# Two chunks of k ahead of ssm_k, four products on GpSimd, 512-column cosine products and a deferred spectrum step

## Chip, cores, metric

The kernel runs on one core of a Trainium2 chip. The metric is device time of one execution in microseconds (us); lower is better. The kernel before has a median of 221.08 us over 3 runs (220.58 to 221.51). Profiles give a span some 2 us shorter than the time (in the profiled run of the changed kernel 221.3 against 223.38).

## The reference, cut

```python
k_pad = jnp.pad(k, ((0, 0), (ks - 1, 0), (0, 0)))                  # B, S, D = 1, 2048, 512; ks = 4
for t in range(ks):                                                  # short causal filter: the "taps"
    k_shift = k_shift + k_pad[:, t:t + S, :] * shift_k[:, ks - 1 - t][None, None, :]
kv = k_shift * v
kv_f = rfft(pad(kv, S)); kf_f = rfft(pad(ssm_k, S))                  # length 4096, along the sequence
y = irfft(kv_f * kf_f)[:, :S] + kv * ssm_D                           # cut: casts and transposes
h = x + layernorm(x) * y                                             # x = q
h2 = h + relu(layernorm(h) @ w1) @ w2                                # Dff = 1376
```

The Fourier transforms are matrix products in two stages with sine and cosine tables. Everything below concerns the first third: loads, taps, transposes, the spectrum of ssm_k, and the start of the product of both spectra.

Names used below: in the profile PE is TensorE (PEld its weight loads), DVE, ACT and POOL are VectorE, ScalarE and GpSimd, and SPq is the queue that issues the loads. A bank is one of the buffers into which TensorE writes its sums. k0 to k3 and v0 to v3 are the four chunks of 512 tokens of k and v; a load "lands" when its data is there. kvx is k after the taps, times v; kfl and xfl are ssm_k and kvx after the transposes. A halved window is a stretch in which the records show TensorE's clock at half.

## The kernel before: the parts concerned

```python
psum = pl.push("psF", bufs=8, space=PSUM)                            # eight one-bank buffers
...
warm = psum.tile([P, CH], F32, tag="ps", name="warm")
for _ in range(11):
    nc.tensor.matmul(out=warm[:], lhsT=wz[:, 0:P], rhs=wz[:], start=True, stop=True)
for c, src in ((0, "k"), (0, "s"), (0, "v"), (1, "k"), (1, "v"), (2, "k"), (2, "v"), (3, "k"), (3, "v")):
    ...   # "s": ssm_k, a plain load; "k" and "v": transposing loads of 512 tokens, all on one queue
...
def taps(u):                                     # 16 units: chunk c of k, quarter rg of the columns
    c, rg = divmod(u, DC)
    ps = psum.tile([P, CH], F32, tag="ps", name="pkv")
    for j in range(KS):
        nc.tensor.matmul(out=ps[:], lhsT=wdiag[:, rg, j, :], rhs=kT[:, rg, CH * c + 16 - j:CH * c + CH + 16 - j],
                         start=(j == 0), stop=(j == KS - 1))
    return u, ps
# times_v(u, ps): kvx = ps * vT on DVE, which frees the bank
...
first = [taps(u) for u in range(4)]
for q in range(8):                               # 64 transposes of ssm_k, copied to kfl by DVE and ACT
    to_rows(lambda n: skv[:, :, :, n], q, kfl, "DDDDADDA"[q])
    if q == 1:
        for u, ps in first:
            times_v(u, ps)
...
for gb in range(8):                              # the other 12 units, between the groups of ssm_k's first stage
    for u in ((4, 5), (6,), (7, 8), (9,), (10, 11), (12,), (13, 14), (15,))[gb]:
        times_v(*taps(u))
    group_k(gb)                                  # 128 short products in four banks, then four copies
...
for q in range(8):                               # 64 transposes of kvx, copied to xfl
    to_rows(lambda n: kvc[:, n // 4, :, n % 4], q, xfl, "DDADDADD"[q])

def spectrum_k(kp):                              # ssm_k's second stage: 16 steps
    ks = slice(2 * kp, 2 * kp + 2)
    ps = [psum.tile([P, 2, 256], F32, tag="ps", name=f"ps2k{s}") for s in range(2)]
    for s in range(2):
        stage2(ps[s], lambda c: a1k[:, c, :], kp, s)     # four 256-column products each
    nc.vector.tensor_tensor(out=kf[:, 0, :, ks], in0=ps[0][:].rearrange("p k j -> p j k"), in1=dcol, op=ALU.add)
    nc.scalar.copy(out=kf[:, 1, :, ks], in_=ps[1][:].rearrange("p k j -> p j k"))

for gb in range(8):                              # two steps, then a group of kv's first stage
    spectrum_k(2 * gb)
    spectrum_k(2 * gb + 1)
    stage1(gb, xfl, lambda o, j, n: a1x[:, o, :, j:j + n], "ADAD", 2 if gb == 7 else 1)
```

GpSimd makes the table cn as eight negated pieces of cs, and last the small tables dre and dim. `a1x` overwrites `a1k` in place, so a group must wait for the spectrum steps that read its columns.

## Time and profile before

| | before |
|---|---|
| time, 3 runs | 221.08 us (220.58 to 221.51) |
| profiled span, mean granted clock | 218.7 us, 0.990 |
| landings k0, ssm_k, v0, k1, v1, k2, v2, k3, v3 | 6.5, 12.2, 14.5, 17.0, 20.3, 22.5, 24.7, 28.6, 32.0 us |
| transposes of kvx start | 36.98 us |
| first add of the spectrum | 41.55 us |
| first product of both spectra (t) on DVE | 65.04 us |

The prediction shows the page's shares and the stages. Two readings are added here. First, the page's row of the granted TensorE clock, one digit for each fortieth of the span (5.5 us), 9 or above being full:

```profile
PEclk9969999999999999999999999999999999999999
```

One slice is reduced: the clock records put a halved window at 13.1 to 16.5 us, inside the transposes of ssm_k (the only other begins at 217.9, where the program ends). Second, the marks by which the stages are compared later, from the timeline (start, length, engine, line, operation, count, and in brackets the idle time before it and what ended it): the transposes of kvx, DVE's copies of them to xfl, the first add of the spectrum, the first t.

```profile
36.98 3.77 PE L217 MATMUL pst<-ident,kvx 128*128 128x128 bf16 x64 [0.17 <-PE ps L244]
37.66 3.97 DVE L221 TENSOR_SCALAR xfl<-pst 128x512 int32<-128x512 int32 x6
41.55 1.42 DVE L330 TENSOR_TENSOR kf<-ps2k,dtab 128x512 fp32r<-128x512 f32 x2
65.04 4.08 DVE L365 TENSOR_TENSOR t<-u,kf 128x704 fp32r<-128x704 f32 x5 [1.27 <-ACT usb L361]
```

From kvx to t the kernel takes 65.04 - 36.98 = 28.06 us, of which 4.57 go to the first add.

### The profile page before, as it was taken

To read this page: it belongs to the slowest core of one execution; us is meant where nothing else is said; L and a number is where in the kernel's file an instruction comes from. 1 tells how busy PE (TensorE), PEld (TensorE's weight loads), DVE (VectorE), ACT (ScalarE), POOL (GpSimd) and SP (SyncE) were. 2 spreads that over 40 slices of the span, in tenths; PEclk is the share of its full clock that TensorE was granted. 3 is DMA by queue.
4 is the path that set the end of the run, shared out by engine and by line. 5 is a ranking of instruction groups with operands and counts; after the bars stand their busy time and mean duration, and the time that the engine had idled before them with its cause. 6 is when DMAs were issued, how large, how long until landed. Compare 5 with 4: busy or idle time off the path is not lost.

```text
span 218.7 us, 7281 instructions
## 1 busy us (share of the span) xinstructions
PE 202.8 (93%) x3103; PEld 139.4 (64%) x3122; DVE 148.2 (68%) x304; ACT 127.7 (58%) x242; POOL 65.9 (30%) x99
## 2 busy tenths in 40 slices
PE   7879889999979999989987899999999999999993
PEld 2276446999968999879965587444444444444442
DVE  7978868899979999957968779742973257130032
ACT  2587858788867888858966699003740066206500
POOL 6059920000029999969200120210021002000000
PEclk9969999999999999999999999999999999999999
DMA  6999960000000000059970000332022110421012
GB/s 96 383 224 191 142 136 7 3 4 3 6 3 0 1 0 3 1 134 216 305 252 3 6 0 3 42 77 55 24 52 63 42 47 0 96 57 42 0 42 54
DMA packets 30383, 15.40 MB, mean 70 GB/s; under 512 B 25520, under 2 KB 29072, under 8 KB 30224
## 3 DMA queue, kind: packets, MB, share of 16 engines
q1 hardware_dynamic: 29520, 14.76, 29.9%
q8 instruction: 24, 0.39, 0.8%
q10 hardware_dynamic: 832, 0.20, 0.4%
q14 instruction: 7, 0.06, 0.1%
HBM read 7.08 MB, written 2.10 MB: 42 GB/s over the span
## 4 chain that ended last, share of the span: by engine, by line
PE 83%; ACT 6%; DMA 4%; issue 2%; DVE 2%; SPq 1%; ACTq 0%
PE ps2m L568 17%; PE ps1m L556 16%; PE pz L482 8%; PE psi L449 7%; PE psy L375 7%; PE pst L217 5%; PE ps L244 4%; PE pkv L271 4%; PE ps2k L259 4%; DMA pre<-in_A_ssm_k_dram 4%; PE ps2k L261 3%; PE u L259 3%; PE u L261 3%; ACT ecore L143 1%; SPq L121 1%
## 5 line engine op out<-in xcount | busy, mean ns | idle before, releaser
L556 PE MATMUL ps1m<-hlnT,w 128*128 128x512 bf16 (+3 forms) x219 | 39.5, 336 | 0.3
L558 ACT ACTIVATE h1T<-ps1m 128x512 bf16<-128x512 f32 (+3 forms) x55 | 27.4, 514 | 21.2 <-PE ps1m L556 20.3
L568 PE MATMUL ps2m<-w,h1T 128*128 128x512 bf16 (+3 forms) x177 | 38.9, 366 | 0.7 <-issue 0.3
L570 DVE TENSOR_TENSOR o<-ps2m,xh 128x512 bf16<-128x512 f32 (+1 forms) x17 | 11.1, 659 | 38.1 <-PE ps2m L568 37.6
L556 PEld LDWEIGHTS <-w 128*128 128x128 bf16 (+1 forms) x220 | 21.7, 100 | 17.6 <-issue 1.4
L568 PEld LDWEIGHTS <-h1T 128*128 128x128 bf16 (+1 forms) x187 | 17.6, 98 | 21.2 <-issue 3.1
L365 DVE TENSOR_TENSOR t<-u,kf 128x704 fp32r<-128x704 f32 x32 | 26.7, 887 | 2.9 <-ACT usb L361 2.6
L365 POOL TENSOR_TENSOR t<-usb,kf 128x320 fp32r<-128x320 f32 x32 | 28.1, 922 | 1.4 <-ACT usb L361 1.0
L493 ACT CAST zt<-pz 128x512 bf16<-128x512 f32 x16 | 8.4, 592 | 29.2 <-PE pz L482 29.2
L482 PE MATMUL pz<-bp,ecore 32*32 32x128 f32 x1024 | 22.5, 384 | 2.3 <-issue 1.4
L231 ACT CAST a<-ps 128x512 fp32r<-128x512 f32 (+1 forms) x42 | 21.2, 575 | 4.3 <-PE ps L244 4.2
L502 POOL TENSOR_SCALAR rstd<-mv 128x4 f32<-128x4 f32 (+1 forms) x7 | 1.6, 232 | 70.3 <-DVE mv L509 70.3
L482 PEld LDWEIGHTS pz<-bp,ecore 32*32 32x32 f32 x1024 | 14.2, 103 | 9.4 <-issue 5.4
L231 ACT CAST kf<-psy 128x512 fp32r<-128x512 f32 x30 | 17.4, 640 | 1.7 <-PE psy L375 0.2
L233 DVE CAST a<-ps 128x512 fp32r<-128x512 f32 (+1 forms) x26 | 16.1, 647 | 3.1 <-PE ps L244 2.9
L507 DVE BATCH_NORM_STATS2 st<-xh 128x6 f32<-128x512 bf16 x28 | 17.4, 680 | 0.0
L449 PE MATMUL psi<-dre,kf 128*128 128x256 f32 x64 | 15.5, 284 | 0.9 <-ACT kf L231 0.9
L375 PE MATMUL psy<-t,ipos 128*128 128x512 f32 x48 | 15.8, 391 | 0.0
L271 PE MATMUL pkv<-kT,wdiag 128*128 128x512 bf16 x56 | 14.8, 380 | 0.8 <-DMA kT<-in_A_k_dram 0.3
L449 PE MATMUL psi<-dim,kf 128*128 128x256 f32 x64 | 15.4, 283 | 0.0
L209 POOL TENSOR_SCALAR c2n<-c2s 128x512 fp32r<-128x512 f32 x8 | 11.9, 1559 | 8.9 <-ACT c2s L177 8.9
L449 PEld LDWEIGHTS psi<-dre,kf 128*128 128x128 f32 x64 | 12.3, 192 | 1.3 <-ACT kf L231 1.3
(115 smaller groups left out, 377.0 us busy)
## 6 DMA issues: line engine op xcount, KB each, us to landing
pre<-in_A_ssm_k_dram SPq DMA_DIRECT2D x1, 2048.0 KB, 8.7
out_dram<-o SPq DMA_DIRECT2D x58, 32.0 KB, 1.6
xh<-in_A_q_dram SPq DMA_DIRECT2D x4, 384.0 KB, 6.8
w<-in_B_w_dram SPq DMA_DIRECT2D x1, 1376.0 KB, 12.7
w<-in_B_w_dram SPq DMA_DIRECT2D x1, 1280.0 KB, 15.8
xh<-in_A_q_dram SPq DMA_DIRECT2D x4, 128.0 KB, 2.8
hlnT<-hln SPq DMA_TRANSPOSE x12, 2.4
w<-in_B_w_dram SPq DMA_DIRECT2D x1, 96.0 KB, 15.4
```

The costliest lines, as they stand in the source:

```text
L231: nc.scalar.copy(out=o, in_=i)
L233: nc.vector.tensor_copy(out=o, in_=i)
L259: nc.tensor.matmul(out=ps[:, kk, :], lhsT=w_re[:, k1, :], rhs=a_in(col(k1, 0)), start=True, stop=False, skip_group_check=True)
L271: nc.tensor.matmul(out=ps[:], lhsT=wdiag[:, rg, j, :], rhs=kT[:, rg, CH * c + 16 - j:CH * c + CH + 16 - j], start=(j == 0), stop=(j == KS ...
L365: eng.tensor_tensor(out=t[:, :, j, :], in0=in0.unsqueeze(1).to_broadcast([P, 2, n, 2]), in1=kfr[:, :, j, ks], op=ALU.mult)
L375: nc.tensor.matmul(out=psy[:], lhsT=m_[:], rhs=t_.rearrange("p j k -> p (j k)"), start=first, stop=not first)
L449: nc.tensor.matmul(out=ps[:, i, :], lhsT=kf[:, c, 4 * m:4 * m + 4, :].rearrange("p r k -> p (r k)"), rhs=d[:].rearrange("p a b -> p (a b)" ...
L482: nc.tensor.matmul(out=pz[32 * a:32 * a + 32, r4, l4, :], lhsT=ecore[rows, rho, n2, :], rhs=rhs, start=(rho == 0), stop=(rho == 1), tile_p ...
L507: nc.vector.bn_stats(out=st[:, t % 4, :], in_=xh[:, t, :])
L556: nc.tensor.matmul(out=ps1[:fsz, :], lhsT=w1[:, c, fc * P:fc * P + fsz], rhs=hlnTs[sc][:, c, part], start=(c == 0), stop=(c == DC - 1))
L558: nc.scalar.activation(out=h1s[sc][:fsz, fc, part], in_=ps1[:fsz, :], func=ACT.Relu)
L568: nc.tensor.matmul(out=ps2[:], lhsT=h1s[sc][:ksz, fc, i * P:(i + 1) * P], rhs=w2[:ksz, fc, ds], start=(fc == 0), stop=(fc == NFC - 1))
```

## The change

The intent: TensorE stands idle until ssm_k lands (2.08 us ahead of 12.29). With k0 and k1 both loaded before it, eight units of taps instead of four fill that time. Their eight banks must be freed before the transposes: ACT copies four of them out and GpSimd multiplies those by v. In the spectrum, the two products that use the cosine table become one of 512 columns, so a step needs one tile of two banks; and its last step ("the spare eighth") goes behind kv's last group, for which `a1` gets eight more columns.

The core of the diff; left out are renamed buffers, the split of the memory for partial sums into two pools (psS, psX), the placing of t and of a later table in spare space, the second half of the cosine table, now made ahead of the transposes, the dealing of the copies of ssm_k's groups (eight letters "AADAAADA" become "ADAADADA"), and kv's last group, which is no longer cut in two:

```diff
-    for c, src in ((0, "k"), (0, "s"), (0, "v"), (1, "k"), (1, "v"), (2, "k"), (2, "v"), (3, "k"), (3, "v")):
+    for c, src in ((0, "k"), (1, "k"), (0, "s"), (1, "v"), (0, "v"), (2, "k"), (2, "v"), (3, "k"), (3, "v")):
...
-    first = [taps(u) for u in range(4)]
+    first = [taps(u) for u in range(8)]
+    ck = early.tile([P, DC, CH], F32, name="ck")
+    for u, ps in first[0:4]:
+        nc.scalar.copy(out=ck[:, u, :], in_=ps)
...
     for h in range(8):
         nc.gpsimd.tensor_single_scalar(out=cn[:, hs, :], ...)
-        if h == 0:
+        if h == 1:
+            for u in range(4):
+                times_v(u, ck[:, u, :], nc.gpsimd)
+        if h == 7:
             nc.gpsimd.tensor_copy(out=dtab[:], ...)
...
-        to_rows(lambda n: skv[:, :, :, n], q, kfl, "DDDDADDA"[q])
+        to_rows(lambda n: skv[:, :, :, n], q, kfl, "DDDDDDAA"[q])
         if q == 1:
-            for u, ps in first:
+            for u, ps in first[4:8]:
                 times_v(u, ps)
...
-        for u in ((4, 5), (6,), (7, 8), (9,), (10, 11), (12,), (13, 14), (15,))[gb]:
+        for u in ((8, 9), (10,), (11,), (), (12,), (13,), (14,), (15,))[gb]:
...
-        ps = [psum.tile([P, 2, 256], F32, tag="ps", name=f"ps2k{s}") for s in range(2)]
-        for s in range(2):
-            stage2(ps[s], lambda c: a1k[:, c, :], kp, s)
+        ps = psK.tile([P, 2, 2, 256], F32, tag="pk", name="ps2k")          # psK: two buffers
+        for kk in range(2):
+            k1 = 2 * kp + kk
+            both = a1k.rearrange("p (o c k) j -> p o k c j", c=2, k=4)[:, k1 // 4, k1 % 4]
+            nc.tensor.matmul(out=ps[:, kk], lhsT=cc[:, k1, :], rhs=both, start=True, stop=False, ...)
+            nc.tensor.matmul(out=ps[:, kk, 0], lhsT=cs[:, k1, :], rhs=a1k[:, col(k1, 1), :], ...)
+            nc.tensor.matmul(out=ps[:, kk, 1], lhsT=cn[:, k1, :], rhs=a1k[:, col(k1, 0), :], ...)
...
         spectrum_k(2 * gb)
-        spectrum_k(2 * gb + 1)
-        stage1(gb, xfl, lambda o, j, n: a1x[:, o, :, j:j + n], "ADAD", 2 if gb == 7 else 1)
+        if gb < 7:
+            spectrum_k(2 * gb + 1)
+        stage1(gb, xfl, lambda o, j, n: a1x[:, o, :, j:j + n], "ADAD", ...)
+    spectrum_k(15)
```

More of the change, by code (lines that the diff above doesn't have):

```diff
@@ L90, with bank @@
     kvp = pl.push("kvp", side="right")
-    psum = pl.push("psF", bufs=8, space=PSUM)
+    psS = pl.push("psS", bufs=4, space=PSUM)
+    psX = pl.push("psX", bufs=4, space=PSUM, side="right")
+    turn = [0]
+    def bank():
+        turn[0] += 1
+        return (psX if turn[0] % 8 in (1, 2, 3, 4) else psS).tile([P, 512], F32, tag="ps", name="ps")[:]
     wsh = consts.tile([P, DC, KS], BF16, name="wsh")
     nc.sync.dma_start(out=wsh[:], in_=A_shift_k.rearrange("(r p) j -> p r j", p=P))
-    pre = slotA.tile([P, 4096 + 2048], I32, tag="A", name="pre")
+    pre = slotA.tile([P, 4096 + 2 * 2048], I32, tag="A", name="pre")
     skf = pre[:, 0:4096].bitcast(BF16)
@@ L110 @@
     nc.vector.memset(wz[:], 1.0)
-    warm = psum.tile([P, CH], F32, tag="ps", name="warm")
+    warm = bank()
     for _ in range(11):
-        nc.tensor.matmul(out=warm[:], lhsT=wz[:, 0:P], rhs=wz[:], start=True, stop=True)
+        nc.tensor.matmul(out=warm, lhsT=wz[:, 0:P], rhs=wz[:], start=True, stop=True)
     nc.vector.memset(kT[:, :, 0:16], 0.0)
-    for c, src in ((0, "k"), (0, "s"), (0, "v"), (1, "k"), (1, "v"), (2, "k"), (2, "v"), (3, "k"), (3, "v")):
+    for c, src in ((0, "k"), (1, "k"), (0, "s"), (1, "v"), (0, "v"), (2, "k"), (2, "v"), (3, "k"), (3, "v")):
         ts = slice(CH * c, CH * c + CH)
@@ L159 @@
     nc.gpsimd.iota(r3[:], pattern=[[1, 64]], base=0, channel_multiplier=0)
-    r2 = early.tile([P, 32, 64], I32, name="w_r")
-    nc.gpsimd.iota(r2[:], pattern=[[2, 32], [128, 64]], base=1, channel_multiplier=0)
+    r2 = pre[:, 6144:8192].rearrange("p (k n) -> p k n", n=64)
+    nc.gpsimd.iota(r2, pattern=[[2, 32], [128, 64]], base=1, channel_multiplier=0)
     n1c = early.tile([P, 1], F32, name="n1c")
@@ L178, in table, with taps, times_v @@
                                  scale=hsc[:, dp:dp + 1], bias=hbi[:, dp:dp + 1])
+    kvx = early.tile([P, 16, DC, 32, 4], BF16, name="kvx")
+    def taps(u):
+        c, rg = divmod(u, DC)
+        ps = bank()
+        for j in range(KS):
+            nc.tensor.matmul(out=ps, lhsT=wdiag[:, rg, j, :], rhs=kT[:, rg, CH * c + 16 - j:CH * c + CH + 16 - j],
+                             start=(j == 0), stop=(j == KS - 1))
+        return u, ps
+    def times_v(u, ps, eng=nc.vector):
+        c, rg = divmod(u, DC)
+        split = "p (a h l) -> p a h l"
+        eng.tensor_tensor(out=kvx[:, :, rg, 8 * c:8 * c + 8, :].rearrange("p h a l -> p a h l"),
+                                in0=ps.rearrange(split, h=16, l=4),
+                                in1=vTs[c][:, rg, :].rearrange(split, h=16, l=4), op=ALU.mult)
     t1 = early.tile([P, 64], I32, name="f1_t")
@@ L192 @@
     _sin(dsc[:], t3[:], 64)
+    first = [taps(u) for u in range(8)]
+    ck = early.tile([P, DC, CH], F32, name="ck")
+    for u, ps in first[0:4]:
+        nc.scalar.copy(out=ck[:, u, :], in_=ps)
     tsn = pre[:, 4096:6144].rearrange("p (k n) -> p k n", n=64)
-    _turns(nc, tsn, r2[:], n2c[:], 8192, False)
+    _turns(nc, tsn, r2, n2c[:], 8192, False)
     table(cs, tsn)
@@ L201 @@
     nc.vector.tensor_copy(out=f1lo[:], in_=f1d[:])
-    _turns(nc, r2[:], r2[:], n2c[:], 8192, True)
-    table(cc, r2[:], (0,))
+    _turns(nc, r2, r2, n2c[:], 8192, True)
+    table(cc, r2)
     dtab = consts.tile([P, 8, DC, 8], BF16, name="dtab")
@@ L209 @@
         nc.gpsimd.tensor_single_scalar(out=cn[:, hs, :], in_=cs[:, hs, :].bitcast(F32), scalar=-1.0, op=ALU.mult)
-        if h == 0:
+        if h == 1:
+            for u in range(4):
+                times_v(u, ck[:, u, :], nc.gpsimd)
+        if h == 7:
             nc.gpsimd.tensor_copy(out=dtab[:], in_=d0[:].rearrange("p r (o g) -> p o r g", g=8))
     def to_rows(cols, q, fl, eng):
-        pst = psum.tile([P, 8, P], BF16, tag="ps", name="pst")
+        pst = bank().bitcast(BF16).rearrange("p (i x) -> p i x", i=8)
         for i in range(8):
@@ L221, in to_rows @@
             nc.vector.tensor_single_scalar(out=fl[:].rearrange("p g d n c -> p g d (n c)").bitcast(I32)[:, :, :, qs],
-                                           in_=pst[:].bitcast(I32).rearrange("p i (d g) -> p g d i", d=2),
+                                           in_=pst.bitcast(I32).rearrange("p i (d g) -> p g d i", d=2),
                                            scalar=0, op=ALU.bitwise_or)
@@ L233, in copy, with stage1 @@
             nc.vector.tensor_copy(out=o, in_=i)
-    def stage1(gb, fl, a_out, engs, parts=1):
-        n = 8 // parts
-        for h in range(parts):
-            pss = [psum.tile([P, n, 64], F32, tag="ps", name=f"ps1_{r}") for r in range(4)]
+    def stage1(gb, fl, a_out, engs, get):
+        n = 8
+        for h in range(1):
+            pss = [get().rearrange("p (g c) -> p g c", g=8) for r in range(4)]
             for gi in range(n):
@@ L248, in stage1 @@
                 copy(engs[(4 * gb + rg) % len(engs)], a_out(gb, 8 * rg + n * h, n),
-                     pss[rg][:].rearrange("p g c -> p c g"))
+                     pss[rg].rearrange("p g c -> p c g"))
     def col(k1, c):
@@ L262, in stage2 @@
                              skip_group_check=True)
-    kvx = early.tile([P, 16, DC, 32, 4], BF16, name="kvx")
-    def taps(u):
-        c, rg = divmod(u, DC)
-        ps = psum.tile([P, CH], F32, tag="ps", name="pkv")
-        for j in range(KS):
-            nc.tensor.matmul(out=ps[:], lhsT=wdiag[:, rg, j, :], rhs=kT[:, rg, CH * c + 16 - j:CH * c + CH + 16 - j],
-                             start=(j == 0), stop=(j == KS - 1))
-        return u, ps
-    def times_v(u, ps):
-        c, rg = divmod(u, DC)
-        split = "p (a h l) -> p a h l"
-        nc.vector.tensor_tensor(out=kvx[:, :, rg, 8 * c:8 * c + 8, :].rearrange("p h a l -> p a h l"),
-                                in0=ps[:].rearrange(split, h=16, l=4),
-                                in1=vTs[c][:, rg, :].rearrange(split, h=16, l=4), op=ALU.mult)
     def group_k(gb):
-        stage1(gb, kfl, lambda o, j, n: a1k[:, :, 32 * o + j:32 * o + j + n], "AADAAADA")
-    first = [taps(u) for u in range(4)]
+        stage1(gb, kfl, lambda o, j, n: a1k[:, :, 32 * o + j:32 * o + j + n], "ADAADADA", bank)
     kfl = early.tile([P, 32, 2, 64, 2], BF16, name="kfl")
@@ L289 @@
     for q in range(8):
-        to_rows(lambda n: skv[:, :, :, n], q, kfl, "DDDDADDA"[q])
+        to_rows(lambda n: skv[:, :, :, n], q, kfl, "DDDDDDAA"[q])
         if q == 1:
-            for u, ps in first:
+            for u, ps in first[4:8]:
                 times_v(u, ps)
-    table(cc, r2[:], (1,))
     dre = consts.tile([P, 2, P], F32R, name="dre")
@@ L299 @@
     nc.gpsimd.memset(dim[:].bitcast(F32), 0.0)
-    a1 = slotA.tile([P, 64 * 256], F32R, tag="A", name="a1")
-    a1k = a1[:].rearrange("p (c j) -> p c j", j=256)
-    a1x = a1[:].rearrange("p (o c j) -> p o c j", o=8, j=32)
+    a1 = slotA.tile([P, 72 * 256], F32R, tag="A", name="a1")
+    a1k = a1[:, 8 * 256:72 * 256].rearrange("p (c j) -> p c j", j=256)
+    a1x = a1[:, 0:64 * 256].rearrange("p (o c j) -> p o c j", o=8, j=32)
     for gb in range(8):
-        for u in ((4, 5), (6,), (7, 8), (9,), (10, 11), (12,), (13, 14), (15,))[gb]:
+        for u in ((8, 9), (10,), (11,), (), (12,), (13,), (14,), (15,))[gb]:
             times_v(*taps(u))
@@ L316 @@
     kvc = kvx[:].rearrange("p h r a l -> p h (r a) l")
+    turn[0] = 0
     for q in range(8):
@@ L322 @@
     kf = slotB.tile([P, 2, 256, 32], F32R, tag="B", name="kf")
+    pl.pop("psX")
+    psK = pl.push("psK", bufs=2, space=PSUM, side="right")
     dcol = dtab[:].rearrange("p o r g -> p (o r g)").unsqueeze(2).to_broadcast([P, 256, 2])
@@ L326, in spectrum_k @@
         ks = slice(2 * kp, 2 * kp + 2)
-        ps = [psum.tile([P, 2, 256], F32, tag="ps", name=f"ps2k{s}") for s in range(2)]
-        for s in range(2):
-            stage2(ps[s], lambda c: a1k[:, c, :], kp, s)
-        nc.vector.tensor_tensor(out=kf[:, 0, :, ks], in0=ps[0][:].rearrange("p k j -> p j k"), in1=dcol, op=ALU.add)
-        nc.scalar.copy(out=kf[:, 1, :, ks], in_=ps[1][:].rearrange("p k j -> p j k"))
+        ps = psK.tile([P, 2, 2, 256], F32, tag="pk", name="ps2k")
+        for kk in range(2):
+            k1 = 2 * kp + kk
+            both = a1k.rearrange("p (o c k) j -> p o k c j", c=2, k=4)[:, k1 // 4, k1 % 4]
+            nc.tensor.matmul(out=ps[:, kk], lhsT=cc[:, k1, :], rhs=both, start=True, stop=False,
+                             skip_group_check=True)
+            nc.tensor.matmul(out=ps[:, kk, 0], lhsT=cs[:, k1, :], rhs=a1k[:, col(k1, 1), :], start=False, stop=True,
+                             skip_group_check=True)
+            nc.tensor.matmul(out=ps[:, kk, 1], lhsT=cn[:, k1, :], rhs=a1k[:, col(k1, 0), :], start=False, stop=True,
+                             skip_group_check=True)
+        nc.vector.tensor_tensor(out=kf[:, 0, :, ks], in0=ps[:, :, 0].rearrange("p k j -> p j k"), in1=dcol, op=ALU.add)
+        nc.scalar.copy(out=kf[:, 1, :, ks], in_=ps[:, :, 1].rearrange("p k j -> p j k"))
     for gb in range(8):
         spectrum_k(2 * gb)
-        spectrum_k(2 * gb + 1)
-        stage1(gb, xfl, lambda o, j, n: a1x[:, o, :, j:j + n], "ADAD", 2 if gb == 7 else 1)
-    pl.pop("psF")
+        if gb < 7:
+            spectrum_k(2 * gb + 1)
+        stage1(gb, xfl, lambda o, j, n: a1x[:, o, :, j:j + n], "ADAD",
+               lambda: psS.tile([P, 512], F32, tag="ps", name="ps")[:])
+    spectrum_k(15)
+    pl.pop("psK")
+    pl.pop("psS")
     pl.pop("xfp")
     prod = pl.push("prod", bufs=3, side="right")
-    psum = pl.push("psP", bufs=2, space=PSUM)
+    psU = pl.push("psU", bufs=2, space=PSUM)
+    psY = pl.push("psY", bufs=2, space=PSUM, side="right")
     ipos = prod.tile([P, P], F32R, name="ipos", bufs=1)
@@ L356, in product @@
         for s in range(2):
-            u = psum.tile([P, 2, 256], F32, tag=f"u{s}", name=f"u{s}")
+            u = psU.tile([P, 2, 256], F32, tag=f"u{s}", name=f"u{s}")
             stage2(u, lambda c: a1x[:, :, c, :], kp, s)
@@ L361, in product @@
             nc.scalar.copy(out=usb[:], in_=uj[:, po, :])
-            t = prod.tile([P, 2, 256, 2], F32R, tag=f"t{s}", name=f"t{s}")
+            if kp % 3 < 2:
+                t = prod.tile([P, 2, 256, 2], F32R, tag=f"t{s}", name=f"t{s}", bufs=2)[:]
+            else:
+                o = 64 * 256 + 1024 * s
+                t = a1[:, o:o + 1024].rearrange("p (a j k) -> p a j k", a=2, k=2)
             for eng, in0, j in ((nc.vector, uj[:, dv, :], dv), (nc.gpsimd, usb[:], po)):
@@ L372, in finish @@
         for s, (a, b, m) in enumerate(((tr[:, 0], ti[:, 1], ineg), (tr[:, 1], ti[:, 0], ipos))):
-            psy = psum.tile([P, 512], F32, tag=f"psy{s}", name=f"psy{s}")
+            psy = psY.tile([P, 512], F32, tag=f"psy{s}", name=f"psy{s}")
             for m_, t_, first in ((ipos, a, True), (m, b, False)):
@@ L385 @@
         finish()
-    pl.pop("psP")
+    pl.pop("psU")
+    pl.pop("psY")
     pl.pop("prod")
@@ L423, in ec_product @@
         nc.gpsimd.iota(r4[:], pattern=[[16, 4], [1, 4], [64, 32]], base=4 * q, channel_multiplier=0)
-        ect[q] = [tmpc.tile([P, 4, 4, 32], I32, tag=f"ec_t{c}", name="ec_t", bufs=4) for c in range(2)]
+        ect[q] = [bpx[:, 16384 + 512 * q:16384 + 512 * q + 512].bitcast(I32).rearrange("p (a l n) -> p a l n", a=4, l=4),
+                  tmpc.tile([P, 4, 4, 32], I32, tag="ec_t", name="ec_t", bufs=4)[:]]
         for c in range(2):
-            nc.gpsimd.tensor_scalar(out=ect[q][c][:], in0=r4[:], scalar1=k1o[:], scalar2=(6144.0, 4096.0)[c],
+            nc.gpsimd.tensor_scalar(out=ect[q][c], in0=r4[:], scalar1=k1o[:], scalar2=(6144.0, 4096.0)[c],
                                     op0=ALU.mult, op1=ALU.add)
@@ L430, in ec_turns @@
         for c in range(2):
-            nc.vector.tensor_single_scalar(out=ect[q][c][:], in_=ect[q][c][:], scalar=8191, op=ALU.bitwise_and)
+            nc.vector.tensor_single_scalar(out=ect[q][c], in_=ect[q][c], scalar=8191, op=ALU.bitwise_and)
     def ec_sin(q, c):
-        _sin(ecore[:, c].rearrange("p (a q l) n -> p q a l n", a=4, l=4)[:, q], ect[q][c][:], 8192, neg=c == 1)
+        _sin(ecore[:, c].rearrange("p (a q l) n -> p q a l n", a=4, l=4)[:, q], ect[q][c], 8192, neg=c == 1)
     def row_stats(mv, t):
@@ L438, in row_stats @@
         nc.vector.bn_aggr(out=mv[:, t, :], in_=st[:, t % 4, :])
+    bpx = slotA.tile([P, 72 * 256], F32, tag="A", name="bp")
+    bp = bpx[:, 0:64 * 256].rearrange("p (m r d n) -> p m r d n", m=64, r=2, d=2)
     for q in range(4):
         ec_product(q)
-    bp = slotA.tile([P, 64, 2, 2, 64], F32, tag="A", name="bp")
     for b in range(32):
```

## The prediction

> **What bounds the kernel now.** I read the page's shares first, then the chain that ended last, then busy time by stretch, then the timeline of the first 68 us, where the change lies.
>
> From the page: TensorE carries the span, so a gain must shorten TensorE's work or its waits.
>
> ```profile
> PE 202.8 (93%) x3103; PEld 139.4 (64%) x3122; DVE 148.2 (68%) x304; ACT 127.7 (58%) x242; POOL 65.9 (30%) x99
> PE 83%; ACT 6%; DMA 4%; issue 2%; DVE 2%; SPq 1%; ACTq 0%
> ```
>
> Busy time by stretch (length; then PE, weight loads, DVE, ACT, POOL; granted clock; DMA share; GB/s). The reader is to see the one TensorE hole (10.2 to 12.3), the reduced clock just after it, a stretch to 37 that is TensorE work with small gaps, and a spectrum stretch (40.5 to 62.2) where DVE is nearly full too.
>
> ```profile
> 10.20:12.30 2.10, 0.01 (x2) 0.01 (x1) 2.00 (x2) 2.10 (x2) 0.00 (x0) 1.00 1.13 283
> 12.30:18.50 6.20, 6.20 (x63) 6.20 (x64) 5.05 (x9) 4.20 (x4) 5.07 (x5) 0.72 1.19 234
> 18.50:37.00 18.50, 16.32 (x556) 8.87 (x564) 14.05 (x22) 13.94 (x25) 10.37 (x15) 1.00 0.75 114
> 37.00:40.50 3.50, 3.50 (x63) 3.50 (x64) 3.36 (x6) 3.12 (x7) 0.00 (x0) 1.00 0.00 0
> 40.50:62.20 21.70, 21.67 (x615) 20.19 (x613) 19.79 (x32) 18.27 (x31) 0.00 (x0) 1.00 0.02 4
> 67.40:95.40 28.00, 27.17 (x170) 24.07 (x168) 25.72 (x32) 23.87 (x57) 26.39 (x35) 1.00 0.00 1
> ```
>
> Timeline (start, length): four units of taps, the wait for ssm_k, the next load issues, and DVE standing for the last chunk of v.
>
> ```profile
> 6.58 3.62 PE L271 MATMUL pkv<-kT,wdiag 128*128 128x512 bf16 x16 [0.27 <-DMA kT<-in_A_k_dram]
> 12.29 6.47 PE L217 MATMUL pst<-ident,pre 128*128 128x128 bf16 x64 [2.08 <-DMA pre<-in_A_ssm_k_dram]
> 16.49 3.46 SPq L121 DMA_TRANSPOSE kT<-in_A_k_dram  x1
> 24.40 3.87 SPq L123 DMA_TRANSPOSE vT<-in_A_v_dram  x1
> 32.09 0.69 DVE L278 TENSOR_TENSOR kvx<-pkv,vT 128x512 bf16<-128x512 f32 x1 [0.97 <-DMA vT<-in_A_v_dram]
> ```
>
> The trace's landing records give k0 6.5, ssm_k 12.2, v0 14.5, k1 17.0, v1 20.3, k2 22.5, v2 24.7, k3 28.6, v3 32.0. From 3.5 to about 32 the DMA engines have work nearly without a break: the first 32 us are a load stream of fixed total length.
>
> Timeline of the spectrum: DVE's add and ACT's copy of one step overlap; 256-column products start 0.12 us apart. Matmuls of 512 columns (third and fourth line) start 0.23 apart.
>
> ```profile
> 60.68 0.28 PE L259 MATMUL ps2k<-a,c2c 128*128 128x256 f32 x1
> 60.80 0.28 PE L261 MATMUL ps2k<-a,c2s 128*128 128x256 f32 x1
> 67.38 0.39 PE L375 MATMUL psy<-t,ipos 128*128 128x512 f32 x1
> 67.61 0.40 PE L375 MATMUL psy<-t,ineg 128*128 128x512 f32 x1
> 60.88 0.69 ACT L331 CAST kf<-ps2k 128x512 fp32r<-128x512 f32 x1
> 60.98 1.28 DVE L330 TENSOR_TENSOR kf<-ps2k,dtab 128x512 fp32r<-128x512 f32 x2
> 63.92 0.36 PE L259 MATMUL u<-a,c2c 128*128 128x256 f32 x1 [0.98 <-DVE a L233]
> ```
>
> [...]the window from 9.7 to 13.1 was 38% busy and the next one, to 16.5, ran at half clock; that is why the 64 transposes took 6.47 us there and 3.77 us at 37. [...]so a doubled matmul saves almost nothing. The trace: 0.12 and 0.23 us. [...]Before, add and copy read separate banks and overlap. [...]The landings above are in order of issue.
>
> **The change, part by part.**
>
> *Loads.* The order becomes k0, k1, ssm_k, v1, v0, k2, v2, k3, v3. k1 ahead of ssm_k costs one transpose load, 2.2 to 2.5 us apiece by the issue times and the landing steps, so ssm_k lands at about 14.6 instead of 12.2, v1 at 16.9, v0 at 20.3. k2 is sixth in both orders and v3 last: they still land at about 22.5 and 32.
>
> *Taps.* A unit is 4 matmuls, 0.85 us at full clock. Units 4 to 7 (3.4 us) move into the hole before ssm_k: TensorE works from 6.6 to about 13.5. The transposes then start at 14.6 at full clock. Their fourth to seventh banks need v1's products on DVE (16.9 + 4 x 0.69 = 19.7), so TensorE ends them at about 20.2 (18.5 before) and DVE the kfl copies at about 22.4. ACT's four copies (0.57 each) and four sine halves (2.1 each) run from 7.5 to about 19.2, before its two kfl pieces.
>
> *Behind that.* Eight units and eight groups are left. One group costs 0.61 of matmuls and 0.42 of gap: 1.03. Before: 18.51 + 12 x 0.85 + 8 x 1.03 = 36.95, as the trace has it. After, unit 8 needs k2: 22.5 + 8 x 0.85 + 8 x 1.03 = 37.5. So the moved work does not return: TensorE stands from 20.2 to 22.5 instead. A second limit is v3 on DVE: 32.0 + four products (0.69) + the four to six copies (0.69) between them also gives about 37.6. The kvx transposes start 0.6 to 0.7 later than at 36.98; DVE, with two copies of the last group behind its last product instead of one, starts theirs about 1.3 later.
>
> *Spectrum.* Per k1, four products of 0.121 = 0.484 become 0.228 + 2 x 0.121 = 0.470: 0.014 x 32 = 0.45 us of TensorE in all. DVE needs per group 2 x 0.68 + 2 x 0.645 = 2.65 of the 2.72 us period. The scheduled instructions show ACT's copy now waiting for DVE's add, as both read both banks. With two buffers of two banks, a buffer is free about 0.06 + 0.66 us later; followed through two groups this still gives 2.7 to 2.75 us a group. No gain here, no loss.
>
> *Spare eighth.* The last spectrum step (0.94) moves behind the last stage-1 group, into the gap of which 0.98 is shown as a wait for DVE. But DVE's last add and ACT's last copy then stand ahead of the first product: their 0.66 each take back most of it. I count 0.7 to 1.0 us of the late start as recovered. The product stage stays at its 1.86 us a step on TensorE.
>
> *Sum.* Late by 1.3 at the kvx copies, less about 1.0: +0.3 us. To this comes the clock: the window from 19.9 to 23.4 would hold 0.3 + 0.85 us of TensorE work, 33%[...]. A halved window at 23.4 to 26.8, and perhaps 22.5 to 23.4, costs up to 1.9 us of TensorE work and leaves about +1.8 at the end. [...]I give that one half: 0.5 x 0.3 + 0.5 x 1.8 = about +1. Something for overlaps that I have not seen: +0.8, so 221.9 us.
>
> **The rivals.** *The intent holds:* 3.4 us of taps saved against 2.3 us of later ssm_k, and 1 us at the spare eighth: 219. For it: TensorE idles at 10.2. Against: k2 and v3 keep their place in a stream that never pauses. *GpSimd becomes the bound:* its products need v0 (20.3); four at about 1.5 us (an estimate from 0.92 us for 320 elements), six negations of 1.56, the copy of dtab and 3.7 us of small tables end at about 39.5, while the first spectrum add, which waits for GpSimd, is at 42 to 43.[...] *The serial add and copy stretch the spectrum period* to about 2.9: 1.5 us more, 223.
>
> **Range and chances.** 219.6 to 224.2 holds the intent's best and the halved clock. 2% is 4.4 us: no single mechanism reaches it. Faster 0.04, same 0.90, slower 0.06.
>
> **What would show it.** ssm_k landing at 14 to 15.5 and transposes at full clock; TensorE standing on k2 at about 22.5 ahead of unit 8; the kvx transposes at 37.3 to 39; a spectrum period of 2.65 to 2.8 with ACT waiting for DVE; the gap ahead of the first product under 0.7. Wrong, if k2 or v3 lands over 1.5 us away from 22.5 and 32, if the kvx transposes start before 36.5, or if the spectrum period falls under 2.6.

## The result and the profile after

The changed kernel takes 223.41 us (median of 3 runs, 223.38 to 223.91) and is correct. The ratio is 1.0113 (95% interval 1.0073 to 1.0154): the same within 2%, and slower by about 1%. A ratio here is the mean time of one kernel's fast runs over that of the other's of the same rounds, so not quite the ratio of the medians quoted. Run again at the end, it gave 222.76 us and 1.0128 (1.0068 to 1.0188).

| | before | after | difference |
|---|---|---|---|
| profiled span, clock | 218.7 us, 0.990 | 221.3 us, 0.982 | +2.6 |
| ssm_k lands | 12.2 | 14.3 | +2.1 |
| k2 lands | 22.5 | 22.1 | -0.4 |
| v3 lands | 32.0 | 28.4 | -3.6 |
| transposes of kvx start | 36.98 | 39.12 | +2.14 |
| first add of the spectrum | 41.55 | 44.06 | +2.51 |
| first t on DVE | 65.04 | 67.26 | +2.22 |

So 2.14 of the 2.6 us are lost before the spectrum starts, and from there to the first t nothing is given back. From the page after (shares, clock by slices, chain that ended last):

```profile
PE 204.3 (92%) x3072; PEld 138.1 (62%) x3090; DVE 147.4 (67%) x302; ACT 126.8 (57%) x240; POOL 70.5 (32%) x103
PEclk9999699999999999999999799999999999999998
PE 77%; SPq 7%; DVE 4%; ACT 4%; issue 3%; DMA 3%; DVEq 0%
```

The reduced clock has moved from the third slice to the fifth, and another stands in the 23rd. The chain now has 7% of load issues on the sync queue, 1% before: the end follows the order of the loads. The timeline after: transposes of ssm_k, the taps of units 8 and 9 in two lines, the transposes of kvx and DVE's copies of them.

```profile
14.39 6.14 PE L251 MATMUL ps<-ident,pre 128*128 128x128 bf16 x64 [1.06 <-DMA pre<-in_A_ssm_k_dram]
22.09 0.61 PE L195 MATMUL ps<-kT,wdiag 128*128 128x512 bf16 x1 [1.57 <-DMA kT<-in_A_k_dram]
22.92 2.73 PE L195 MATMUL ps<-kT,wdiag 128*128 128x512 bf16 x6 [0.22 <-issue]
39.12 3.74 PE L251 MATMUL ps<-ident,kvx 128*128 128x128 bf16 x64
40.42 3.67 DVE L255 TENSOR_SCALAR xfl<-ps 128x512 int32<-128x512 int32 x6
```

TensorE stands 1.57 us on k2, and then works on units 8 and 9 until 25.6: 3.5 us for work that took 1.9 elsewhere. Busy time by stretch shows why (length; PE, weight loads, DVE, ACT, POOL; clock; DMA share; GB/s):

```profile
20.50:22.10 1.60, 0.03 (x2) 0.01 (x1) 1.11 (x2) 1.39 (x3) 1.60 (x2) 0.99 0.91 56
22.10:25.50 3.40, 3.18 (x7) 1.00 (x8) 0.69 (x1) 0.00 (x0) 3.40 (x4) 0.50 1.20 249
```

The first is the wait, the second a halved window that falls on eight 512-column products. Before, the halved window fell on the 64 transposes and cost little: they took 6.47 us there and 6.14 after at full clock. Behind them DVE's copies and products stand without a gap (15.37 to 21.60 in after), so I take these to set their pace; that is argued, not tested.

In the spectrum, DVE's add and ACT's copy no longer overlap: here the first two steps.

```profile
44.06 1.48 DVE L355 TENSOR_TENSOR kf<-ps2k,dtab 128x512 fp32r<-128x512 f32 x2
44.78 1.42 ACT L356 CAST kf<-ps2k 128x512 fp32r<-128x512 f32 x2 [1.70 <-DVE kf L355]
```

The copy starts when the first add is done (it waits 1.70 us, the last of it for DVE); before, the two ran from their own banks, and at the same time (60.88 and 60.98 in the prediction's timeline). The period is 2.75 us a group against 2.73, so the time is neither lost nor won. At the end of the spectrum stand the first product, the spare step's add, its copy, and the first t:

```profile
65.93 0.35 PE L293 MATMUL u<-a,c2c 128*128 128x256 f32 x1 [0.38 <-DVE a L267]
65.70 0.68 DVE L355 TENSOR_TENSOR kf<-ps2k,dtab 128x512 fp32r<-128x512 f32 x1
66.42 0.62 ACT L356 CAST kf<-ps2k 128x512 fp32r<-128x512 f32 x1 [0.87 <-DVE kf L355]
67.26 3.29 DVE L400 TENSOR_TENSOR t<-u,kf 128x704 fp32r<-128x704 f32 x4 [0.87 <-ACT usb L391]
```

TensorE's gap before the first product fell from 0.98 to 0.38 us as intended. But the first t needs ACT's copy usb of that product, and ACT has the spare step's copy ahead of it, until about 67.0.

### The profile page after: what moved, and what is told of

It is laid out like the page before. It is cut to its first block, busy times and chain, and to the rows that moved or that the text cites. A ratio compares the mean times of both kernels' runs of the same rounds, so it can differ in the third digit from the quotient of the medians.

```text
span 221.3 us, 7200 instructions
## 1 busy us (share of the span) xinstructions
PE 204.3 (92%) x3072; PEld 138.1 (62%) x3090; DVE 147.4 (67%) x302; ACT 126.8 (57%) x240; POOL 70.5 (32%) x103
## 4 chain that ended last, share of the span: by engine, by line
PE 77%; SPq 7%; DVE 4%; ACT 4%; issue 3%; DMA 3%; DVEq 0%
PE ps2m L606 17%; PE ps1m L594 16%; PE pz L520 10%; PE psi L487 7%; PE psy L410 6%; SPq L131 4%; PE ps L278 4%; PE ps2k L349 3%; PE ps L195 3%; PE u L293 3%; PE u L295 3%; DMA kT<-in_A_k_dram 3%; SPq L129 2%; PE ps L251 2%; DVE a L267 1%
## 5 line engine op out<-in xcount | busy, mean ns | idle before, releaser
L594 PE MATMUL ps1m<-hlnT,w 128*128 128x512 bf16 (+3 forms) x219 | 39.5, 336 | 0.3
L606 PE MATMUL ps2m<-w,h1T 128*128 128x512 bf16 (+3 forms) x177 | 38.9, 366 | 0.7 <-issue 0.3
L265 ACT CAST a<-ps 128x512 fp32r<-128x512 f32 x36 | 19.1, 597 | 8.0 <-issue 4.6
L400 POOL TENSOR_TENSOR t<-usb,kf 128x320 fp32r<-128x320 f32 x22 | 19.7, 936 | 2.0 <-ACT usb L391 1.8
L267 DVE CAST a<-ps 128x512 fp32r<-128x512 f32 x28 | 18.2, 685 | 3.1 <-PE ps L278 3.1
L400 DVE TENSOR_TENSOR t<-u,kf 128x704 fp32r<-128x704 f32 x22 | 18.4, 885 | 2.1 <-ACT usb L391 2.1
L195 PE MATMUL ps<-kT,wdiag 128*128 128x512 bf16 x57 | 16.2, 410 | 2.7 <-DMA kT<-in_A_k_dram 1.6
L356 ACT CAST kf<-ps2k 128x512 fp32r<-128x512 f32 x16 | 10.4, 648 | 5.9 <-DVE kf L355 5.8
L349 PE MATMUL ps2k<-a,c2c 128*128 128x512 f32 x32 | 13.5, 423 | 0.2
```

The costliest lines, as they stand in the source:

```text
L195: nc.tensor.matmul(out=ps, lhsT=wdiag[:, rg, j, :], rhs=kT[:, rg, CH * c + 16 - j:CH * c + CH + 16 - j], start=(j == 0), stop=(j == KS - 1))
L265: nc.scalar.copy(out=o, in_=i)
L267: nc.vector.tensor_copy(out=o, in_=i)
L349: nc.tensor.matmul(out=ps[:, kk], lhsT=cc[:, k1, :], rhs=both, start=True, stop=False, skip_group_check=True)
L400: eng.tensor_tensor(out=t[:, :, j, :], in0=in0.unsqueeze(1).to_broadcast([P, 2, n, 2]), in1=kfr[:, :, j, ks], op=ALU.mult)
L594: nc.tensor.matmul(out=ps1[:fsz, :], lhsT=w1[:, c, fc * P:fc * P + fsz], rhs=hlnTs[sc][:, c, part], start=(c == 0), stop=(c == DC - 1))
```

## A second measure: spans by the number of halved windows

Each run lists its span and mean granted clock. A halved window is 3.41 us long in the clock records (13.11 to 16.52 in before, 22.08 to 25.49 in after), so a run has (1 - clock) x 2 x span / 3.41 of them, to within the fraction at the end of the program. That sorts the fast runs of all rounds, with the mean span in us (number of runs):

| kernel | 0 halved | 1 | 2 | 3 |
|---|---|---|---|---|
| before | 218.80 (2) | 218.11 (18) | 219.12 (4) | 219.63 (6) |
| after (both times) | none | 220.47 (4) | 221.22 (4) | 222.90 (1) |
| e3_loads_only | none | 220.80 (2) | 221.30 (2) | 222.20 (2) |
| e4_spectrum_only | none | 218.30 (2) | 218.80 (4) | none |
| e2_k2_first | 218.24 (5) | 219.30 (1) | none | none |
| e5_fill_spread | 219.92 (5) | none | 221.80 (1) | none |
| e6_spread | 218.35 (2) | 218.30 (2) | 219.40 (1) | none |
| e7_pool | 217.55 (2) | 217.63 (3) | 219.30 (1) | none |
| e10_best | 217.00 (3) | 217.15 (2) | 218.70 (1) | none |

Left out are one fast run of e6 with four (220.7) and the kernels that are not compared here. About half of the scatter of one kernel goes with this number (48% of the variance of the span in the 30 fast runs of before, 218.6 to 222.1 us, beside the experiments). Kernels can be compared at an equal number, though not at an equal place of the window, which only a profiled run shows. The rounds ran on three chips; before at one halved window has 218.10, 218.08 and 218.16 on them, so spans of different rounds can be compared. After stands 2.1 to 2.4 us above before in both columns 1 and 2.

## The experiments

My theory: the loss is the wait for k2 (part 1 of the change), made worse by the halved window that stands behind it (22.1 to 25.5); the spectrum part is neutral. Rivals: GpSimd's products delay the spectrum; the serial add and copy do; v3 ends the stage anyway.

### e1_fill: keep TensorE busy while it waits for k2

```diff
         ps = bank()
+        for _ in range(7 if u == 8 else 0):
+            nc.tensor.matmul(out=ps, lhsT=wz[:, 0:P], rhs=wz[:], start=True, stop=True)
         for j in range(KS):
```

> The changed kernel with seven 512-column matmuls on ones written into unit 8's bank ahead of its taps (thrown away: the first real tap starts the sum anew), so that TensorE is busy between the end of the transposes (20.5 us) and the landing of k2 (22.05 us). Theory (the wait for k2 costs twice: the wait itself, and the halved clock of 22.1 to 25.5 that it brings): no half-clock window there, units 8 and 9 in 1.7 us instead of 3.5, the kvx transposes at about 37.4 instead of 39.1, the total 1.7 us below the changed kernel, about 0.5 us above the kernel before. Rival (DVE's products, which need v2 at 24.3, bound that stretch): the clock is full but the kvx transposes start no earlier than 38.5 and the total falls by less than 0.6 us.

Measured: 222.86 us (222.41 to 224.45), ratio 1.0115 (1.0073 to 1.0156). In the profile the local part came true: the clock is full from 22.1 to 25.5 and the taps of units 8 and 9 take 1.89 us, so the first group starts at 23.91 instead of 25.58.

```profile
22.09 1.89 PE L197 MATMUL ps<-kT,wdiag 128*128 128x512 bf16 x8
22.10:25.50 3.40, 3.40 (x76) 1.56 (x75) 1.49 (x3) 0.80 (x2) 3.40 (x4) 1.00 1.22 249
```

The total did not: the transposes of kvx start at 38.73, only 0.39 earlier. The gain was lost at 28.6 to 30.2, where TensorE waits for no semaphore (weight loads of two groups without taps between them):

```profile
28.35 0.26 PEld L280 LDWEIGHTS <-kfl 32*128 32x128 bf16 x25 [0.51 <-issue]
30.19 0.34 PEld L280 LDWEIGHTS <-kfl 32*128 32x128 bf16 x35 [1.59 <-issue]
```

and a halved window followed at 30.5 to 34.0. So a full clock behind the wait is worth 1.7 us there and then, but here it only moved the hole and the halved window. The expected total was missed. The rival's two numbers came out instead (38.73, and 0.55 us less than after in its first rounds), but its reason, DVE waiting for v2, is not what the profile shows at the hole.

### e2_k2_first: the load that TensorE waits for goes ahead of v0

```diff
-((0, "k"), (1, "k"), (0, "s"), (1, "v"), (0, "v"), (2, "k"), (2, "v"), (3, "k"), (3, "v"))
+((0, "k"), (1, "k"), (0, "s"), (1, "v"), (2, "k"), (2, "v"), (0, "v"), (3, "k"), (3, "v"))
```

> The changed kernel with one edit: v0 is loaded after k2 and v2 instead of before them. Theory: k2 lands at about 18.7 and v2 at 22, TensorE goes from the transposes to unit 8 at about 20.5 with no wait and no halved clock, the kvx transposes start at 35.5 to 36. GpSimd's products then wait for v0 at 24.3 and its work ends at about 41, so the first spectrum add may stand on GpSimd for up to 1 us; the total is 2 to 3.5 us below the changed kernel, 0 to 1.2 below the kernel before. Rival (the place of k2 doesn't matter, the extra work on ACT and GpSimd does): total within 0.6 us of the changed kernel.

Measured: 220.50 us (219.86 to 221.39), ratio 0.9990 (0.9951 to 1.0029): 1.2% better than the change as it was, from the order of the loads alone (the clock that follows from it included: five of its six runs have no halved window), and 2.9 us below it, as expected. k2 lands at 18.7; the taps follow the transposes without a wait, at full clock, and the transposes of kvx start at 36.28.

```profile
14.57 6.16 PE L251 MATMUL ps<-ident,pre 128*128 128x128 bf16 x64 [0.56 <-DMA pre<-in_A_ssm_k_dram]
20.56 1.89 PE L195 MATMUL ps<-kT,wdiag 128*128 128x512 bf16 x8
41.61 1.29 DVE L355 TENSOR_TENSOR kf<-ps2k,dtab 128x512 fp32r<-128x512 f32 x2 [0.36 <-POOL dim L326]
```

The third line shows a new wait: v0 now lands at 24.4, GpSimd's products start later, and the first add waits for GpSimd's last small table. That rival becomes real as soon as the first bound is gone, but it is 0.36 us.

### e3_loads_only and e4_spectrum_only: the two parts apart

e3 has the loads, taps and GpSimd work of after with the spectrum of before; e4 the reverse:

```diff
 # e3: part 1 stays, part 2 goes back
-    psK.tile([P, 2, 2, 256], ...) with 512-column cosine products; spectrum_k(15) behind stage1(7)
+    two one-bank tiles, 256-column products; spectrum_k(15) ahead of stage1(7)
 # e4: part 2 stays, part 1 goes back
-    (0,k),(1,k),(s),(1,v),(0,v),...; first = 8 units, 4 of them by way of ck and GpSimd
+    (0,k),(s),(0,v),(1,k),(1,v),...; first = 4 units, all on DVE
```

> Only the first part of the change (load order, eight units of taps ahead, four of them copied out and multiplied on GpSimd), with the spectrum, the banks and the product stage of the kernel before. Theory (all of the loss is in the first 40 us): kvx transposes at about 39, total 223.0 to 223.8, as slow as the full change. Rival (the spectrum part loses through the copy that waits for the add): total at or under 222.4.

> Only the second part of the change (512-column cosine products into two-bank tiles, last spectrum step behind the last group, spare eighth), with the loads, taps and sine tables of the kernel before. Theory (neutral: 0.45 us of TensorE saved is not the bound, the gap before the first product is filled but add and copy of the last step stand there): total within 0.5 us of the kernel before, spectrum period 2.7 to 2.75 us. Rival A (a gain of its own, hidden in the full change by the loss in the first part): 1 us or more under the kernel before. Rival B (the serial add and copy cost): 0.8 us or more over it.

Measured: e3 222.94 us (222.43 to 224.91), ratio 1.0116 (1.0074 to 1.0158); e4 220.81 us (220.23 to 221.25), ratio 1.0003 (0.9969 to 1.0038). The loads alone make the whole loss, the spectrum part alone is neutral, also at equal numbers of halved windows in the table above. The profiled run of e3 is its slowest (224.91, three halved windows), so I read no stage from it. In e4 the transposes of kvx start at 36.36, the first add at 41.37 and t at 64.58: 28.22 us from kvx to t against 28.06 before.

### e5_fill_spread and e6_spread: no two groups without taps between them

```diff
-((8, 9), (10,), (11,), (), (12,), (13,), (14,), (15,))
+((8, 9), (10,), (11,), (12,), (13,), (14,), (15,), ())
```

e5 is e1 with this, e6 is e2 with this.

> The first experiment (filler matmuls before unit 8) plus one edit: the group without taps is the last and not the fourth, so no two groups of 128 short TensorE instructions follow each other before the last. In the first experiment the clock stayed full where the filler was, but TensorE then stood 1.5 us (wait named issue) after the back-to-back groups[...], and the clock was halved from 30.5 to 34. Theory (the clock costs what the fill takes away[...]): gap under 0.9 us, no halved window before 60 us, kvx transposes at 37.2 to 37.7, total 1.3 to 2 us below the changed kernel, 0.3 to 1 us above the kernel before. Rival (the gap has nothing to do with the rate of instructions): it stays at 1.2 us or more in about the same place.

> The second experiment (v0 behind k2 and v2) plus the same edit, the group without taps last. Theory: kvx transposes at 35.6 instead of 36.3, but the first spectrum add still stands on GpSimd, whose work ends at 41.6 as before; total within 0.4 us of the second experiment. Rival (GpSimd isn't the bound there): total 0.6 us or more below it.

Measured: e5 222.03 us (221.07 to 223.94), ratio 1.0099 (1.0044 to 1.0155); e6 220.56 us (220.38 to 222.83), ratio 1.0037 (0.9989 to 1.0085). The profiled run of e5 has no halved window before its last microsecond, and five of its six runs have none, so here the wait for k2 stands alone:

```profile
22.49 1.89 PE L197 MATMUL ps<-kT,wdiag 128*128 128x512 bf16 x8 [0.25 <-DMA kT<-in_A_k_dram]
37.57 0.47 PEld L280 LDWEIGHTS <-kfl 32*128 32x128 bf16 x51 [1.05 <-issue]
```

I had expected e5 at 0.3 to 1 us over before; it is about 2 us over in these rounds. The hole was not removed: it moved with the pair of groups that has no taps between it, to the last two (1.05 us in e5, 1.14 in e6). What holds TensorE there is not shown. At no halved window e5 has a mean span of 219.92 us and e6 218.35. They differ in the order of the loads and in the filler that stands where k2 is awaited. But e6 is no clean measure: two of its runs stand here, and its profiled one (with four halved windows) waits 1.74 us for k3, which its spread taps need earlier. Against e2, whose profile shows no wait for a load behind the transposes, e5 is 1.68 longer (five runs each, e5's from 219.0 to 221.3). So with the clock full the old place of k2 costs about 1.6 us, to within about 1 us by that scatter. That is close to the wait that the profile shows (1.57 in after), and e5, without the halved clock, is still 1% over before: the wait is most of the loss, the clock the smaller part. e6's total is as expected (220.56 against e2's 220.50); its start of kvx (36.97, in the profiled run) is not.

### e7_pool and e8_all: GpSimd off the path

e7 is e2 with GpSimd's negations ahead of its products; e8 is e7 with the spread of e6 and the copies of ssm_k's groups dealt as before.

```diff
-        if h == 1:
+        if h == 7:
             for u in range(4):
                 times_v(u, ck[:, u, :], nc.gpsimd)
 # e8 also
-"ADAADADA"
+"AADAAADA"
```

> The second experiment plus one edit: GpSimd negates all eight pieces first and multiplies afterwards, so that it does not stand 6 us waiting for v0. Theory: GpSimd is done by about 36, the first spectrum add at about 41.2 and no longer waiting for it (TensorE's lateness takes over after 0.4 us), total 0.3 to 0.7 us below the second experiment. Rival: no change.

> The second experiment with both edits (GpSimd's negations first; the group without taps last) and the eviction pattern of the kernel before (24 of 32 pieces on ACT, 8 on DVE) in the first part's groups. Theory: each removed only uncovered the other's wait, together they take away both: kvx transposes at 35.6 to 36, first spectrum add at 40.2 to 40.7, total 218.9 to 220 us, 1 to 2 us below the kernel before. Rival (another bound follows at once, ACT's evictions): total within 0.5 us of the kernel before.

Measured: e7 219.72 us (219.66 to 221.44), ratio 0.9991 (0.9947 to 1.0034); e8 219.63 us (219.18 to 221.51), ratio 0.9995 (0.9946 to 1.0044). In e7 the first add is at 40.59 and waits for no GpSimd work, so that wait of e2 is gone; at no halved window the span is 217.55 us against e2's 218.24 (two and five runs). By the ratio to before there is no gain, though (0.9991 against e2's 0.9990), which was the rival: a gain of the total is not shown. The 1 to 2 us that I expected of e8 were not there: in its profile TensorE's weight loads wait 1.39 us for k3 (its products 1.28), and the hole at the last pair is 1.03 us.

### e9_spare_only: the spare step without the two-bank tile

```diff
 # e4, with
-        ps = psK.tile([P, 2, 2, 256], F32, tag="pk", name="ps2k")
+        ps = [psK.tile([P, 2, 256], F32, tag=f"pk{s}", name=f"ps2k{s}") for s in range(2)]
+        for s in range(2):
+            stage2(ps[s], lambda c: a1k[:, c, :], kp, s)
```

> Second part of the change alone, without its 512-column products: the spectrum step is that of the kernel before (two one-bank tiles, 256 columns, add and copy side by side), but its last step stands behind the last group, in the layout with the spare eighth. In the kernel before it took 4.57 us from the first kvx transpose to the first spectrum add and 23.49 from there to the first product on DVE; with the full second part 5.01 and 23.21. Theory (the spare eighth gains 0.3 at the end, and the two-bank tile loses 0.4 at the start because the add now waits for the whole step): 4.5 to 4.65 and 23.1 to 23.3, total 0 to 0.6 us below the kernel before. Rival (the serial add and copy are not what costs at the start): 4.9 or more, as in the full second part.

Measured: 221.04 us (218.67 to 222.24; one slow run among them, without it 220.64 against 220.10 for the fast runs of before), ratio 1.0010 (0.9947 to 1.0074), too wide to tell. The answer rests on the stages of one profiled run each:

| from, to (us) | before | after | e4 (both parts of the spectrum) | e9 (spare step alone) |
|---|---|---|---|---|
| kvx transposes to first add | 4.57 | 4.94 | 5.01 | 4.61 |
| first add to first t | 23.49 | 23.20 | 23.21 | 22.86 |
| sum | 28.06 | 28.14 | 28.22 | 27.47 |

The spare step alone saves 0.6 us. In e4 the two-bank tile takes it back: the first add must wait for a whole step on TensorE (0.94 us) instead of half of one, and starts 0.4 us later, after 0.32 of waiting:

```profile
41.37 1.47 DVE L351 TENSOR_TENSOR kf<-ps2k,dtab 128x512 fp32r<-128x512 f32 x2 [0.32 <-PE ps2k L349]
```

From the add to t it takes another 0.34. After differs at the start: its first add (44.06) follows DVE's last copy of kvx without a wait. The stage is longer there because these copies start 1.30 us after the transposes (39.12 to 40.42; before 0.68), behind two copies of the last group. e10, with two one-bank tiles, has 4.89 there too. In e9 the last add and ACT's copy run at the same time again:

```profile
63.25 0.68 ACT L345 CAST kf<-ps2k 128x512 fp32r<-128x512 f32 x1
63.36 0.68 DVE L344 TENSOR_TENSOR kf<-ps2k,dtab 128x512 fp32r<-128x512 f32 x1
```

### e10_best: what the experiments point to

The order of e2, GpSimd as in e7, the spectrum of e9.

> The loads and GpSimd order that were best so far (v0 behind k2 and v2, negations first), with the spectrum step in two one-bank tiles and the spare eighth. Theory: kvx transposes at about 35.7, first add 4.6 later at 40.3, first product at 63.5, total 1 to 1.6 us (0.5 to 0.7%) below the kernel before of the same rounds. Rival (gains in the front are given back later): total within 0.5 us of it.

Measured: 219.00 us (218.46 to 220.56), ratio 0.9952 (0.9903 to 1.0002), as expected, with kvx and t 0.3 us earlier still. The first t is at 63.16, 1.9 us earlier than before:

```profile
35.42 3.74 PE L251 MATMUL ps<-ident,kvx 128*128 128x128 bf16 x64
40.31 1.29 DVE L348 TENSOR_TENSOR kf<-ps2k,dtab 128x512 fp32r<-128x512 f32 x2
63.16 3.29 DVE L393 TENSOR_TENSOR t<-u,kf 128x704 fp32r<-128x704 f32 x4 [0.67 <-ACT usb L384]
```

It is the fastest version: well ahead of after of the same rounds (222.76), and by medians of fast runs 1.1 us ahead of before (220.10), where the interval just touches no difference. At one halved window its span is 217.15 us against 218.11.

### e11_before_fill: fill the hole of the kernel before with dummies

```diff
     first = [taps(u) for u in range(4)]
+    for _ in range(9):
+        nc.tensor.matmul(out=warm[:], lhsT=wz[:, 0:P], rhs=wz[:], start=True, stop=True)
```

> The kernel before with nine 512-column matmuls on ones into the spent warm-up bank between the taps and the first transpose, so that TensorE is busy from 10.2 to 12.2 and the clock of 13.1 to 16.5 stays full. Theory (there DVE's six copies and four products of 0.69 are the bound, so the halved clock cost the kernel before next to nothing): the transposes take 5.3 to 6.2 us, total within 0.5 us of the kernel before. Rival (the halved clock cost it too, as it cost the changed kernel): kvx transposes at 35.5 or earlier, total 1.2 us or more below.

Measured: 223.63 us (220.85 to 224.56; 223.54 in its fast runs), ratio 1.0131 (1.0065 to 1.0196): slower, against both theories. What the profile shows for certain is why there was no gain: the halved window at 13.1 is gone, but the 64 transposes take 5.94 us instead of 6.47, so it had cost only 0.5.

```profile
13.30 5.94 PE L217 MATMUL pst<-ident,pre 128*128 128x128 bf16 x64 [1.29 <-DMA pre<-in_A_ssm_k_dram]
```

Why it is slower is open. In the profiled run, which is counted as a slow one (224.56), the loads are late: ssm_k landed 1.0 us later, v3 at 33.35 instead of 32.0, and DVE waited for chunks of v (1.56, 1.86 and 1.14 us), so kvx and t start 1.3 later. Another 2.7 us is lost behind t, where two halved windows stand (124.9 to 131.7). Late loads come without a filler too: in e9, which has the loads of before, ssm_k landed at 13.27. At no halved window the one run of e11 has 219.0, as before (218.80); but at one its spans are 221.5 and 221.7, over 3 us above before. No run here separates the filler from the delay of the loads.

### e12_after_again: the changed kernel once more

> The changed kernel unedited, on the same chip as these. Theory: 1.0 to 1.2% over the kernel before; its times scatter by 1 us and more[...], and not every execution has the halved window of 22.1 to 25.5. Rival: the first measurement was a chance state, and the ratio is under 1.005.

Measured: 222.76 us (221.86 to 225.03), ratio 1.0128 (1.0068 to 1.0188). The wait for k2 and the halved window behind it are there again:

```profile
22.32 3.55 PE L195 MATMUL ps<-kT,wdiag 128*128 128x512 bf16 x8 [1.74 <-DMA kT<-in_A_k_dram]
```

## Why the prediction was right, and where its steps were off

The time, 223.41 us, lies in the range and the class is as predicted. By its steps:

- **Loads.** ssm_k at 14.6 was 14.3, k2 at 22.5 was 22.1. "v3 last: they still land at about 22.5 and 32" failed for v3: 28.4, outside the 1.5 us that I had set as the mark of an error. It is not a stall of one run: v3 landed at 31.0 to 33.4 in the four profiled runs with the old order (before, e4, e9, e11) and at 28.4 to 30.2 in the five with the new one. The step that failed is "work nearly without a break", a stream "of fixed total length". In before the DMA engines moved only 13 GB/s at 19 to 20 us, 4 at 25 to 26 and 21 at 26 to 27; in after there is one such pause (39 at 21 to 22). So the stream had pauses, and fewer with the new order (two such slices of 1 us fewer, of the 3.6 us by which v3 came earlier); what makes them is open. The second limit built on it, v3 on DVE, did not exist in after (and its sum gives 37.5 only with four copies; with six it is 38.9). That the first limit, k2, gave the same start of kvx is luck.
- **The wait.** "TensorE stands from 20.2 to 22.5 instead" was 20.5 to 22.1, and e5 against e2 and e6 prices it at about 1.6 us with the clock full. This was the heart of the prediction; e2 and e3 show it.
- **The clock.** A halved window at even odds came in both profiled runs of after. Its local cost of 1.67 us (e1: 25.58 to 23.91) is near the 1.9 that I allowed. The 37.5 worked out for kvx without it, with k2 at 22.5, can be held against e5, where the clock is full and k2 lands at 22.45: 38.09. So that sum was 0.6 short; the hole of 1.05 us, in which TensorE waits for no semaphore, was not in it. On the whole span it counts for less: one more halved window goes with 0.75 us in after (220.47 to 221.22). My ground for it, a window 33% busy ahead of it, is not borne out: that window, 18.7 to 22.1, was 55% busy, and the one ahead of the halved window in before, 9.7 to 13.1, 39% (the 38% of the prediction). So a busy share at which the clock falls is not shown. What the runs show is that with the idle time filled the clock of these two places stayed full (e1 from 22.1 to 25.5, e11 from 12.3 to 19.2: granted 1.00). The reading of the clock in the kernel before fails as well: it is not "why the 64 transposes took 6.47 us there and 3.77 us at 37". At full clock they take 5.94 (e11) and 6.14 (after), so the clock explains about 0.5 of these 2.7 us.
- **The spectrum.** "2.7 to 2.75 us a group", neutral, ACT waiting for DVE: measured 2.75, and e4 is neutral at 1.0003.
- **The spare step** is the term that was mis-sized: 0.7 to 1.0 us recovered in the prediction. From the first add to t it is 0.3 (23.49 to 23.20), and from the transposes of kvx to t it is nothing (28.06 to 28.14). The gap on TensorE closed from 0.98 to 0.38 as foreseen. What failed was to value it apart from the two-bank tile: the add and the copy, one after the other, hold back usb at the end. With two one-bank tiles the same stretch is 22.86 (e9) and 22.84 (e10), so the spare step is worth 0.6 and the tile takes 0.34 of it. That the rest vanishes at the start of the stage was foreseen: DVE's copies start later, from 0.68 to 1.30 behind the transposes.
- **The sum.** I had +0.3 us without the halved clock and +1.8 with it (its "+0.8" is the "about +1" taken down for overlaps: 221.08 + 0.8 = 221.9). DVE's copies of kvx start 2.76 us late (37.66 to 40.42), as 1.3 and the clock's 1.5 would have it: in e5, at full clock, they start at 39.41 with k2 0.40 later than in after, which leaves 1.4 for the clock. From there to t 0.54 is recovered in place of 1.0. That makes +2.22 in place of +1.8, and the 0.4 between them is the spare step's. The rest of the distance from 221.9 to 223.4 us is the clock, which I had counted at even odds, and 0.3 us that later stages add (from t to the end 153.7 before and 154.0 after). The second halved window stands there, but it is not shown to be the cause: e2 has 154.0 without one.
- **Rivals.** GpSimd was not the bound: four products took 1.14 us each, not 1.5, and its work ended at 36.0, not 39.5. It became one for 0.36 us in e2. "The intent holds" failed for the reason given against it, but e2 shows that what counted was the place of k2 in the order, which the change could have moved.

## What to carry to other kernels

Work moved into a hole ahead of a late load saved time here only once the next piece of work had its data: after stood 1.57 us on k2, and with k2 ahead of v0 (e2) that wait was gone and the time 2.9 us lower. So when two loads are reordered, look up which load the engine needs right behind the filled hole, and move that one too. What a halved clock cost differed with the work under it: about 0.5 us on 64 transposes, which other work seemed to pace, and 1.7 us locally on eight 512-column products. Merging two tiles into one to save an instruction made their two readers serial (0.34 us at the end of this stage; with two one-bank tiles, in e9, they ran at the same time) and delayed the first reader in e4 (0.4 us), so price the start and the end of such a stage and not its period alone.
